# A forward and backward block on one core: one activation transpose, w_down's last part, the filter copy, the held matmuls and the last stores put at other places

## The chip, the cores and the metric

One core of a Trainium2 chip runs the whole program. The metric is the device time of one execution in microseconds (us). Shown are the median of three runs and one profiled execution, whose trace is the source of every row below. The engines are named as the profile names them: PE (TensorE, matmuls; PEld are its weight loads), DVE (VectorE), ACT (ScalarE), POOL (GpSimd) and SP (SyncE). SP and POOL issue nearly all DMAs here; SPq and POOLq are the issuing instructions in their queues. Each engine works through its own instruction list in a fixed order, and an instruction whose inputs or buffers are not ready holds up all behind it on that engine.

## The reference

The program computes an adaptive-layernorm block, forward and backward. With `x` of 2048 rows by 576, `h = norm(x)*(1+ca)+sa`; `x1 = x + ga*A(h)`, where A is a two-dimensional real FFT, a product with the complex filter `w_r + i*w_i`, and the inverse FFT; `h2 = norm(x1)*(1+cb)+sb`; `out = x1 + gb*B(h2)`, where B is the bilinear unit:

```python
g = jnp.einsum('bsd,df->bsf', x, w_gate)
u = jnp.einsum('bsd,df->bsf', x, w_up)
h = g * u
return jnp.einsum('bsf,fd->bsd', h, w_down)
```

The six vectors sa, ca, ga, sb, cb, gb are `silu(c) @ w_mod`. Outputs are `out` and the gradients of `x`, `w_r`, `w_i`, `w_gate`, `w_up`, `w_down`, `c` and `w_mod` for a given `grad_out`, all in bfloat16. F, the inner width of B, is 4608 = 36 blocks of 128; the 2048 rows are 16 tiles of 128.

## The kernel before

The kernel runs in stages that overlap at their edges.

*Forward stages* (to about 292 us of the span): norm, FFT as matmuls with tables, filter, inverse FFT, second norm; the matmuls for the gradient of the hidden layer are dealt between them.

*Block loop* (`for fb in range(NFB)`): for each of 36 blocks the products `gup` (gate and up), the elementwise `hhT`, `ggT`, `guT` (h, and its gradients toward gate and up), and their turned copies `hh_sf`, `gg_sf`, `gu_sf`, made by SP with a DMA transpose in `turn_items` (L684, L685). The turned copies feed `product(fb, i)` (`u57p`, L615): i = 0 is the gradient of w_down, i = 1 and 2 those of w_gate and w_up. Each finished product of w_gate or w_up is turned back through `woT` and stored by SP (`u57_turn`); one of w_down is stored by SP directly (L636). The pools of `sf` have two buffers each, so block 35 uses those of block 33. For block 35 the three transposes stand under `tc.high_priority(-2 * HEAD_START)`, that is, far back in the order in which the scheduler of the language deals instructions that are ready (`HEAD_START` is 350); elsewhere the offset is 0.

*Sums* (`u8_output`): the gradient of h2 for two blocks at a time, `u8p` (three banks), added by DVE into `acc` (L701).

*Held matmuls.* The products of blocks 34 and 35 (6 x 32 = 192 matmuls) are kept back and used as filler. `lead` deals 48 of them among the last sums, three per tile; `deal` gives the other 144, and then the projection matmuls of tiles 0 to 5 (`proj`, L1187), a fixed quota `q` in each step of the stages 1, 2 and 3, and `in_order` turns the list into PE's order. Held are in the order (34, 0), (35, 0), (34, 1), (35, 1), (34, 2), (35, 2).

*Stage 1* (`t1_norm`, `t1_turn`, `t1_cols`, `t1_rows`; 16 tiles, 19 steps): the backward of the second norm. Its loads `n2c`, `goc`, `yc` (L911) are issued by SP, five buffers each, with the tables RD, G1, BD2, BDA behind those of tiles 1 and 2. POOL stores each tile's `gxr` (L928, called gx below), and `queued_load` places one large POOL load behind a given tile's store: `wd_load` brings parts of w_down (`wdA` for blocks 0 to 14, then `wdB` three times seven blocks: 15, 22 and 29 on), `hl_load` parts of the stored hidden layer, `wn_load` the two halves of the filter copy. `queued` keeps these in the order written. The steps have the norm of tile k, the turn of k−1, the columns of k−2 and the rows of k−3, dealt in reverse.

*Stage 2* (`t2_*`, 19 groups, 24 steps): the backward through the filter. `t2_filter` multiplies with `wn` (`fm`, L214); its result `Ygc` is turned by PE (`try_`) two steps later. `filter_grad` makes the filter's gradient for a group, reading `Xn` (a POOL load, two buffers) and writing into `wn` in place; every fourth group runs in stage 2, the others later. *Stage 3* (`t3_*`, 18 steps): inverse transform and first norm.

*Projection* (16 tiles, the last loop): `u3p` = h by w_down, 72 matmuls per tile; ACT copies it (L1188), DVE makes `pr` (L1191), `of` (L1193) and the output `o` (L1195), POOL stores it (L1196). `x1t` and `got` are loaded by POOL for two tiles at a time, into one buffer each. Between the tiles stand the remaining filter gradients (`more_grads`), four stores of the filter's gradient per tile (`store_grads`, L1167) and the sections of the w_mod gradient (`late`, `section`). `csF` collects `pr` (two tiles late); after the last tile its copy `dgb` (L1214) feeds the last section and the gradient of c.

On chip the left-hand pools after the block loop lie where its buffers lay. Summed from the sizes, the last part of w_down (`oB2`, bytes 93,392 to 101,456 of this region in each partition) lies over the `gg_sf` and `gu_sf` pools, and the `hl` buffers of `hlh` and `hlg` over `h2p` and `gon`; the copy of the filter lies on the right, over `acc1`.

Of the kernel before, what the change touches and what calls it, by code (L numbers as in the profile page):

```python
# [31 lines left out]
HEAD_START = 350  # L32
# [52 lines left out]
def build(ctx, tc, A_x, A_w_r, A_w_i, B_w_gate, B_w_up, B_w_down, c_in, w_mod, grad_out,  # L85
# [3 lines left out]
    NFB = F // 128  # L89
# [24 lines left out]
    MSA, MCA, MGA, MSB, MCB, MGB = range(6)  # L114
# [446 lines left out]
    with ExitStack() as ms:  # L561
# [14 lines left out]
        with ExitStack() as bs:  # L576
# [100 lines left out]
            def turn_items(fb):  # L677
                def turns_():
                    hhT, ggT, guT = trip[fb][2:5]
                    nc.gpsimd.dma_start(hhT_d[:, :, fb, :].rearrange("tp f x -> f tp x"), hhT[:].rearrange("f (tp ti) p -> f tp (ti p)", ti=2))  # L680
                    sfs[fb] = []
                    for pool_, nm, srcT in zip(sfp, ("hh_sf", "gg_sf", "gu_sf"), (hhT, ggT, guT)):
                        sf = pool_.tile([128, NT, 128], BF, name=nm)
                        with tc.high_priority(-2 * HEAD_START if fb == NFB - 1 else 0):  # L684
                            turned = nc.sync.dma_start_transpose(out=sf[:], in_=srcT[:].rearrange("f t p -> f (t p)"))  # L685
                        sfs[fb].append(sf)
                    if fb % FBT == 1 and fb + 3 < NFB:
                        wTs[fb // FBT + 1] = wT_load(fb + 3, [turned.ins] * 5)
                return turns_
# [69 lines left out]
    with ExitStack() as ts:  # L759
# [56 lines left out]
        def deal(held, proj):  # L816
            more, seq = held + proj, list(lead)
            for n, (stage, k, ins) in enumerate(staged):
                seq += ins
                steps = sum(x[:2] == (stage, k) for x in staged)  # L820
                at = sum(x[:2] == (stage, k) for x in staged[:n + 1])
                if stage == 1:
                    q = 8
                else:
                    q = 12 if stage == 2 else 20 if k == 0 else 7
                q = q * at // steps - q * (at - 1) // steps
                seq, more = seq + more[:q], more[q:]
            in_order(seq)
# [32 lines left out]
        def of_rows(d):  # L861
            return [lambda h=h: spread(ones_f[:], d[:, h * 288:(h + 1) * 288]) for h in range(2)]

        def of_sums(d):
            return [lambda h=h: spread(sel[:, h, :], d[:]) for h in range(2)]
# [29 lines left out]
        with ExitStack() as r1:  # L895
# [9 lines left out]
            ld, gyTs, zts = {"order": []}, {}, {}  # L905
# [65 lines left out]
            dcb = diag_rows(tl, csA, csB, 288, "dcb")  # L971
# [22 lines left out]
        def wd_load(f0, n, behind_):  # L994
            k, w = wd_part(f0)
            queued(nc.gpsimd, behind_, w[:, f0 - k:f0 - k + n, :], B_w_down[f0 * 128:(f0 + n) * 128, :].rearrange("(j f) d -> f j d", f=128))
# [10 lines left out]
        def wn_load(c, behind_):  # L1007
            queued(nc.gpsimd, behind_, wn[:, c].rearrange("k a f -> k (a f)"), wn_d[:, c * NT * FP:(c + 1) * NT * FP])

        def queued_load(t, f, *args):  # L1010
            hl = f(*args, ld["gx", t])
            if t < NT - 1:
                in_order([last[nc.gpsimd], ld["gx", t + 1]])
            return hl
# [4 lines left out]
        first_hl = [queued_load(9 + nq, hl_load, nq, nc.gpsimd) for nq in range(3)]  # L1019
        queued_load(12, wd_load, 22, 7)  # L1020
        first_hl.append(queued_load(13, hl_load, 3, nc.gpsimd))
        for c in range(2):
            queued_load(14 + c, wn_load, c)
        wd_load(29, 7, None)
        fg = pool("fg", 2, "right", stack=rA)
        rB = ExitStack()
        A_ = planes(pool("rb", 1, "right", stack=rB), "j_A")
# [125 lines left out]
        rest = [ci for ci in range(NCH) if ci % 4]  # L1153

        def more_grads(t):
            for ci in rest[{5: 0, 7: 3, 9: 7, 11: 11}.get(t, 99):][:3 if t in (5, 11) else 4]:
                with tc.issue_after(ld3["last"]):
                    filter_grad(ci)
            if t == 11:
                for which in range(2):  # L1160
                    for f in (0, DF - 1):
                        nc.gpsimd.tensor_scalar(out=wn[:, which, :, f:f + 1], in0=wn[:, which, :, f:f + 1], scalar1=0.5, scalar2=None, op0=MUL)
# [3 lines left out]
            with tc.issue_after(ins):  # L1166
                nc.gpsimd.dma_start((o2_v, o3_v)[which][:, a0:a0 + 2, :], wn[:, which, a0:a0 + 2, 0:DF])  # L1167

        late = {6: (MSB, of_sums(dsb)), 8: (MCB, of_rows(dcb)), 10: (MGA, of_rows(dga)), 12: (MSA, of_sums(dsa)), 13: (MCA, of_rows(dca))}


        csF = ps_cs.tile([128, 512], FP32, name="csF", tag="csB")
# [1 line left out]
        for tp_ in range(NT // 2):  # L1174
            hls = [first_hl[q] if tp_ == 0 else hl_load(4 * tp_ + q) for q in range(4)]
            x1t = o2p.tile([128, 2, D], BF, name="x1t3", bufs=1)
            nc.gpsimd.dma_start(x1t[:], x1_d[:, 2 * tp_:2 * tp_ + 2, :])
            got = o2p.tile([128, 2, D], BF, name="got3", bufs=1)
            nc.gpsimd.dma_start(got[:], go_v[:, 2 * tp_:2 * tp_ + 2, :])
            for ti in range(2):  # L1180
                t = 2 * tp_ + ti
                mark = traced()
                ob = o2p.tile([128, D], BF, name="ob3")
                for h in range(2):
                    p2 = ps_u3.tile([128, 512], FP32, name="u3p")
                    for fb in range(NFB):
                        mm = nc.tensor.matmul(p2[:, 0:288], lhsT=hls[fb // 9][:, fb % 9, ti * 128:(ti + 1) * 128], rhs=wd_part(fb)[1][:, fb - wd_part(fb)[0], h * 288:(h + 1) * 288], start=(fb == 0), stop=(fb == NFB - 1))  # L1187
                    nc.scalar.copy(ob[:, h * 288:(h + 1) * 288], p2[:, 0:288])  # L1188
                pr = prs[t] = o2p.tile([128, D], BF, name="pr3", bufs=3)
                for h in range(2):  # L1190
                    nc.vector.tensor_tensor(out=pr[:, h * 288:(h + 1) * 288], in0=ob[:, h * 288:(h + 1) * 288], in1=got[:, ti, h * 288:(h + 1) * 288], op=MUL)  # L1191
                of = o2p.tile([128, D], BF, name="of3", bufs=1)
                nc.vector.tensor_tensor(out=of[:], in0=ob[:], in1=gb_h[:], op=MUL)  # L1193
                o0 = o2p.tile([128, D], BF, name="o03", bufs=1)
                nc.vector.tensor_tensor(out=o0[:], in0=of[:], in1=x1t[:, ti, :], op=ADD)  # L1195
                stored = nc.gpsimd.dma_start(o0_v[:, t, :], o0[:])  # L1196
                if t in late:
                    with tc.issue_after(mm.ins):
                        section(*late[t], secp)
                more_grads(t)  # L1200
                if 11 <= t < 15:
                    for k in range(4 * (t - 11), 4 * (t - 10)):
                        store_grads(k, stored.ins)
                if t == 0:
                    add_zero(csF, first=True)
                for d_ in ([t - 2] if t < NT - 1 else [t - 2, t - 1, t]):
                    for h in range(2):
                        if d_ >= 0:
                            colsum(csF, h, prs[d_][:, h * 288:(h + 1) * 288])
                proj[t] = pe_since(mark)  # L1210
# [78 lines left out]
```

## Time and profile before

| what | value |
|---|---|
| runs, median (lowest to highest) | 1581.1 us (1576.41 to 1584.73) |
| profiled execution, own time | 1585.44 us |
| its span | 1583.6 us |
| PE / DVE / ACT / POOL busy | 1516.1 / 1032.1 / 555.7 / 190.0 us |
| granted clock, mean | 0.984 |
| DMA moved | 280.19 MB, mean 177 GB/s |

The stages lie in the span about so: block loop to 1243, sums to 1279, stage 1 to 1347, stage 2 to 1413, stage 3 to 1476, projection to 1567, then the end. In the rows, the first number of a timeline row is its start in us from the span's start, the second its length; what stands in square brackets is the idle time of that engine before it and what ended it. "issue" there means that nothing the profile shows was waited for. A row "DMA to landing" counts from a transfer's issue to its arrival. A PE row's length is longer than the distance between its matmuls, since these are pipelined.

### The profile page before, as it was taken

Reading aid. Unit: us, or ns where it says so; the run is one execution under the profiler, and the core shown is the slowest. Engines: PE = TensorE matmul, PEld = TensorE weight load, DVE = VectorE, ACT = ScalarE, POOL = GpSimd, SP = SyncE. Lnnn points to the kernel's source line nnn. Section 1 sums busy time; section 2 is a strip of 40 time slices with the busy share of each in tenths; the row PEclk is TensorE's granted clock in tenths of the full one; section 3 lists DMA queues with packets and bytes.
Section 4 is the critical chain, followed back from the end, with each engine's and each line's share of the span. In section 5 each row is a group of like instructions: output and inputs, shape, how many; then the busy total and the mean of one; then the engine's idle time right before and its main releaser. Section 6 shows DMA issues by size and latency. Waiting matters only on the chain.

```text
span 1583.6 us, 30053 instructions
## 1 busy us (share of the span) xinstructions
PE 1516.1 (96%) x11300; PEld 1030.4 (65%) x11306; DVE 1032.1 (65%) x2622; ACT 555.7 (35%) x1141; POOL 190.0 (12%) x301
## 2 busy tenths in 40 slices
PE   6999989999999999999999999999999789799996
PEld 4665533567666666666666666666766567588774
DVE  7866743666666666666666666666666666578765
ACT  6667722322222222222222222222222246467222
POOL 0001212101010000101001010100100312210224
PEclk9999999999999999999999999999999989899998
DMA  9869998778877685785768777675866769654866
GB/s 316 275 196 242 285 212 230 151 149 144 151 147 154 128 168 115 158 157 118 161 135 155 144 151 132 146 162 117 161 128 129 203 170 291 173 198 146 304 209 166
DMA packets 488195, 280.19 MB, mean 177 GB/s; under 512 B 408913, under 2 KB 459218, under 8 KB 487026
## 3 DMA queue, kind: packets, MB, share of 16 engines
q1 hardware_dynamic: 460898, 177.69, 52.8%
q0 software_dynamic: 27152, 100.59, 21.7%
q8 instruction: 88, 1.44, 0.4%
q14 instruction: 57, 0.47, 0.1%
HBM read 108.33 MB, written 82.31 MB: 120 GB/s over the span
## 4 chain that ended last, share of the span: by engine, by line
PE 77%; DVE 7%; DMA 6%; issue 6%; ACT 2%; POOL 1%; SPq 1%; DVEq 0%; ACTq 0%; POOLq 0%
PE u57p L615 26%; PE u8p L696 17%; PE gup L667 16%; PE u4p L426 7%; PE gup L662 2%; PE u3p L1187 2%; DMA Xn<-xn_d 1%; DMA hh_sf<-hhT 1%; DMA wdB<-in_B_w_down_dram 1%; PE zp L952 1%; DVE pr L880 1%; PE zp L364 1%; DVE ln_st L162 1%; DMA x1t<-x_d 1%; DMA wdT<-wdn 1%
## 5 line engine op out<-in xcount | busy, mean ns | idle before, releaser
L701 DVE TENSOR_TENSOR acc<-acc,u8p 128x288 f32<-128x288 f32 x1088 | 489.2, 453 | 326.9 <-PE u8p L696 326.7
L696 PE MATMUL u8p<-wT,ggT 128*128 128x288 bf16 x1152 | 329.3, 287 | 1.8 <-DVE acc L701 1.8
L696 PE MATMUL u8p<-wT,guT 128*128 128x288 bf16 x1152 | 328.8, 287 | 0.0
L667 PE MATMUL gup<-h2T,wgu 128*128 128x512 bf16 x1152 | 294.9, 379 | 0.0
L617 ACT CAST so<-u57p 128x288 bf16<-128x288 f32 x216 | 86.0, 398 | 534.8 <-PE u57p L615 526.8
L615 PE MATMUL u57p<-gon,hh_sf 128*128 128x288 bf16 x1152 | 189.6, 287 | 10.6 <-DMA hh_sf<-hhT 10.6
L615 PE MATMUL u57p<-h2p,gg_sf 128*128 128x288 bf16 x1152 | 189.8, 286 | 0.0
L615 PE MATMUL u57p<-h2p,gu_sf 128*128 128x288 bf16 x1152 | 188.2, 286 | 0.0
L667 PEld LDWEIGHTS <-wgu 128*128 128x128 bf16 x1152 | 109.5, 98 | 98.8 <-issue 17.1
L696 PEld LDWEIGHTS <-ggT 128*128 128x128 bf16 x1152 | 113.0, 98 | 67.7 <-issue 14.0
L426 PE MATMUL u4p<-goT,wdT 128*128 128x512 bf16 x656 | 152.7, 382 | 0.6 <-DVE goT L398 0.5
L696 PEld LDWEIGHTS <-guT 128*128 128x128 bf16 x1152 | 113.1, 98 | 56.2 <-issue 2.5
L615 PEld LDWEIGHTS <-hh_sf 128*128 128x128 bf16 x1152 | 112.8, 98 | 39.6 <-DMA hh_sf<-hhT 11.2
L1187 PEld LDWEIGHTS <-hl 128*128 128x128 bf16 x1152 | 108.7, 98 | 36.5 <-issue 12.4
L615 PEld LDWEIGHTS <-gu_sf 128*128 128x128 bf16 x1152 | 112.3, 98 | 28.5
L615 PEld LDWEIGHTS <-gg_sf 128*128 128x128 bf16 x1152 | 112.1, 98 | 28.1
L669 ACT CAST gT<-gup 128x512 bf16<-128x512 f32 x144 | 84.4, 586 | 130.7 <-PE gup L667 130.7
L426 PEld LDWEIGHTS <-wdT 128*128 128x128 bf16 x656 | 61.6, 98 | 74.6 <-issue 10.3
L669 ACT CAST uT<-gup 128x512 bf16<-128x512 f32 x144 | 84.3, 585 | 73.5 <-PE gup L667 73.5
L1187 PE MATMUL u3p<-wdB,hl 128*128 128x288 bf16 x672 | 99.3, 288 | 11.1 <-DMA wdB<-in_B_w_down_dram 11.1
L680 POOL DMA_DIRECT2D hhT_d<-hhT x36 | 33.2, 921 | 481.9 <-DVE hhT L671 452.9
L152 ACT CAST ghh_st<-u4p 128x512 bf16<-128x512 f32 x88 | 50.8, 586 | 73.7 <-PE u4p L426 72.8
(362 smaller groups left out, 1701.9 us busy)
## 6 DMA issues: line engine op xcount, KB each, us to landing
ghhT_d<-ghh_st POOLq DMA_DIRECT2D x36, 512.0 KB, 4.5
ghh<-ghhT_d POOLq DMA_DIRECT2D x36, 512.0 KB, 7.5
hhT_d<-hhT POOLq DMA_DIRECT2D x36, 512.0 KB, 6.5
hl<-hhT_d SPq DMA_DIRECT2D x28, 576.0 KB, 6.5
out_dram<-woT SPq DMA_DIRECT2D x72, 128.0 KB, 2.0
wdn<-in_B_w_down_dram SPq DMA_DIRECT2D x18, 288.0 KB, 3.8
out_dram<-so SPq DMA_DIRECT2D x36, 144.0 KB, 2.7
wgu<-in_B_w_gate_dram SPq DMA_DIRECT2D x18, 256.0 KB, 3.2
```

The lines of the kernel that those rows point to most:

```text
L152: nc.scalar.copy(dst, src)
L162: nc.vector.bn_stats(out=st[:, t, h, :], in_=xt[:, t, h * 288:(h + 1) * 288])
L426: nc.tensor.matmul(pt[:], lhsT=wdTs[k][:, j, m, :], rhs=goT[:, 4 * sb4:4 * sb4 + 4, m, :], start=(m == 0 and n == 5), stop=(m == n - 1))
L615: mm = nc.tensor.matmul(pw[0][:, 0:288], lhsT=sf[:, t, :], rhs=rhs_n[:, t, h * 288:(h + 1) * 288], start=(t == 0), stop=(t == NT - 1))
L617: nc.scalar.copy(so[:, h * 288:(h + 1) * 288], pw[0][:, 0:288])
L662: nc.tensor.matmul(pts[-1][:], lhsT=wgu[r, 8, jw * 128:(jw + 1) * 128], rhs=h2T[r, 4 * sb4:4 * sb4 + 4, 4, :], start=True, stop=False)
L667: nc.tensor.matmul(pts[k][:], lhsT=wgu[:, 4 * wi_ + m, jw * 128:(jw + 1) * 128], rhs=h2T[:, ts_, m, :], start=False, stop=(m == 3))
L669: nc.scalar.copy((gT, uT)[wi_][:, ts_, :], pts[k][:])
L680: nc.gpsimd.dma_start(hhT_d[:, :, fb, :].rearrange("tp f x -> f tp x"), hhT[:].rearrange("f (tp ti) p -> f tp (ti p)", ti=2))
L696: nc.tensor.matmul(pu[:, 0:288], lhsT=l_, rhs=r_, start=(k == 0), stop=(k == len(mms) - 1))
L701: nc.vector.tensor_tensor(out=dst, in0=dst, in1=pu[:, 0:288], op=ADD)
L1187: mm = nc.tensor.matmul(p2[:, 0:288], lhsT=hls[fb // 9][:, fb % 9, ti * 128:(ti + 1) * 128], rhs=wd_part(fb)[1][:, fb - wd_part(fb)[0], h ...
```

## The change

Five places change.

1. In `turn_items`, the turn `hh_sf` of the last block no longer has the lowered priority; `gg_sf` and `gu_sf` keep it.
2. In `deal`, the quota of stage 1 is 11 per step for the first 13 steps, then 8 as before.
3. The POOL loads at the end of stage 1: the last seven blocks of w_down now stand behind the gx store of tile 14, where the first half of the filter copy was; both halves of that copy come behind the store of tile 15 and behind that load.
4. The last three filter gradients and the halving of the filter's edge columns are written at tile 10 instead of 11, and the four stores per tile at tiles 10 to 13 instead of 11 to 14.
5. The last two sections inside the loop are at tiles 11 and 12 instead of 12 and 13.

```diff
-                        with tc.high_priority(-2 * HEAD_START if fb == NFB - 1 else 0):
+                        with tc.high_priority(-2 * HEAD_START if fb == NFB - 1 and nm != "hh_sf" else 0):
...
                 if stage == 1:
-                    q = 8
+                    q = 11 if k < 13 else 8
...
         queued_load(12, wd_load, 22, 7)
         first_hl.append(queued_load(13, hl_load, 3, nc.gpsimd))
-        for c in range(2):
-            queued_load(14 + c, wn_load, c)
-        wd_load(29, 7, None)
+        queued_load(14, wd_load, 29, 7)
+        wn_load(0, ld["gx", 15])
+        wn_load(1, None)
...
-            for ci in rest[{5: 0, 7: 3, 9: 7, 11: 11}.get(t, 99):][:3 if t in (5, 11) else 4]:
+            for ci in rest[{5: 0, 7: 3, 9: 7, 10: 11}.get(t, 99):][:3 if t in (5, 10) else 4]:
...
-            if t == 11:
+            if t == 10:
...
-        late = {6: (MSB, of_sums(dsb)), 8: (MCB, of_rows(dcb)), 10: (MGA, of_rows(dga)), 12: (MSA, of_sums(dsa)), 13: (MCA, of_rows(dca))}
+        late = {6: (MSB, of_sums(dsb)), 8: (MCB, of_rows(dcb)), 10: (MGA, of_rows(dga)), 11: (MSA, of_sums(dsa)), 12: (MCA, of_rows(dca))}
...
-                if 11 <= t < 15:
-                    for k in range(4 * (t - 11), 4 * (t - 10)):
+                if 10 <= t < 14:
+                    for k in range(4 * (t - 10), 4 * (t - 9)):
                         store_grads(k, stored.ins)
```

## The prediction

> **What bounds the kernel now.** I read the waits of TensorE (PE) in the last third first, because its busy share is high everywhere, then cut the span at those waits.
>
> ```profile
> PE u3p L1187 <- DMA wdB<-in_B_w_down_dram: 11.1, 1, 11.1
> PE u57p L615 <- DMA hh_sf<-hhT: 10.2, 1, 10.2
> PE gcp L1225 <- DVE gcd L1221: 6.7, 1, 6.7
> PE spp L858 <- DVE dgb L1214: 4.4, 1, 4.4
> PE u8p L696 <- DVE acc L701: 1.8, 4, 0.7
> ```
>
> The columns are total us, number, longest. Two single waits on transfers, 10.2 and 11.1 us, stand out; the next two are the end of the program. In the windows cut at these waits (PE, PE weight loads, VectorE = DVE, ScalarE = ACT, POOL busy us; then granted clock, DMA share, GB/s):
>
> ```profile
> 1260.50:1270.75 10.25, 0.02 (x1) 0.03 (x2) 2.56 (x7) 0.40 (x1) 6.31 (x6) 0.70 1.03 250
> 1270.75:1279.30 8.55, 8.55 (x54) 6.17 (x55) 3.98 (x9) 0.00 (x0) 0.00 (x0) 0.76 0.20 35
> 1279.30:1346.90 67.60, 65.30 (x648) 52.33 (x649) 45.61 (x122) 42.25 (x99) 16.05 (x27) 1.00 0.83 251
> ...
> 1351.30:1362.40 11.10, 0.04 (x2) 0.01 (x1) 1.77 (x5) 0.28 (x1) 0.94 (x3) 0.59 0.89 200
> 1362.40:1412.90 50.50, 50.38 (x543) 42.50 (x544) 40.51 (x127) 33.20 (x67) 8.13 (x18) 0.95 0.43 146
> 1412.90:1476.00 63.10, 62.99 (x583) 51.89 (x584) 49.14 (x134) 39.16 (x102) 4.83 (x9) 1.00 0.66 213
> ...
> 1566.70:1583.60 16.90, 2.98 (x6) 1.44 (x6) 7.33 (x17) 3.18 (x5) 8.23 (x8) 0.55 0.30 97
> ```
>
> Outside the two waits PE is busy nearly always, so a wait removed is time removed. Each wait also costs something behind it: the clock is 0.76 for 8.55 us after the first (0.24 x 8.55 = 2.05 us lost) and 0.95 for 50.5 us after the second (0.05 x 50.5 = 2.5 us; the 0.59 of the wait itself costs nothing). Together the two are worth 12.3 and 13.6 us.
>
> **Part 1, hh_sf turned earlier.** SyncE's (SP's) queue explains the first wait:
>
> ```profile
> 1243.64 2.24 SPq L685 DMA_TRANSPOSE gu_sf<-guT  x1
> 1245.93 1.31 SPq L911 DMA_DIRECT2D n2c<-n_d  x2
> ...
> 1263.14 0.38 SPq L636 DMA_DIRECT2D out_dram<-so  x1
> 1263.56 3.43 SPq L685 DMA_TRANSPOSE hh_sf<-hhT  x1
> ```
>
> and the list of transfers from 1230 to 1400 us its landing time:
>
> ```profile
> hh_sf<-hhT SPq DMA_TRANSPOSE x1, 7.1
> ```
>
> The turn of hh_sf for block 35 is issued at 1263.56, behind 17 us of norm-stage loads, and lands 7.1 us later. At its normal priority it stands ahead of them: issued about 1245.9, when gu_sf has been issued, landed about 1253. PE wants it at 1260.5, so seven us of slack: the wait goes, −12.3. What is late next are the loads behind it. Each is issued 2.24 (gu_sf's issue) to 3.43 us (its own) later, and VectorE already waits for the first of each:
>
> ```profile
> 1250.97 0.82 DVE L809 SCALAR_TENSOR_TENSOR w<-gn,rstd2g,n2c 128x576 bf16<-128x576 bf16 x1 [0.38 <-DMA n2c<-n_d]
> ...
> 1253.59 0.46 DVE L812 TENSOR_TENSOR u<-u,goc 128x576 bf16<-128x576 bf16 x1 [0.69 <-DMA goc<-in_grad_out_dram]
> ```
>
> Behind L809 on VectorE's queue stand the additions L701 that free the three banks u8p; PE waits for those already (the 1.8 us above), so a later n2c goes through to PE nearly whole. Bounds: 0 if the additions are dealt ahead of the norm, 7.1 if the loads land a whole turn later. I take 2.8, the middle of 2.24 and 3.43. The tables behind them (RD, G1, BD2, BDA) come later by the same 2 to 3 us, and are first read by the columns of stage 1, two steps after PE has left the sums; the turn of gg_sf keeps its place, since the queue's total is the same: nothing for either. Net **−9.5**.
>
> The Trainium skill, "DMA: Bandwidth & Descriptors", section "Queues, rings and completion order", says that on one DMA engine the descriptors of one queue row are consumed in ring order. By that the loads start only when the turn's packets are through, and the 7.1 would apply rather than 2.8: the first rival below.
>
> **Part 2, w_down's last part and the filter copy.** GpSimd's queue (POOL) and PE at the places that decide:
>
> ```profile
> 1330.57 0.54 POOL L928 DMA_DIRECT2D gx_d<-gxr  x1 [3.01 <-DVE gxr L814]
> 1331.10 0.54 POOL L989 DMA_DIRECT2D wn<-wn_d  x1
> ...
> 1334.67 0.55 POOL L928 DMA_DIRECT2D gx_d<-gxr  x1 [2.46 <-DVE gxr L814]
> 1335.20 0.54 POOL L989 DMA_DIRECT2D wn<-wn_d  x1
> ...
> 1346.87 0.97 POOL L989 DMA_DIRECT2D wdB<-in_B_w_down_dram  x1 [10.60 <-PE vp L960]
> ```
>
> ```profile
> 1327.82 0.41 PE L615 MATMUL u57p<-h2p,gu_sf 128*128 128x288 bf16 x2
> ...
> 1343.32 0.53 PE L615 MATMUL u57p<-h2p,gu_sf 128*128 128x288 bf16 x3
> ...
> 1345.92 0.65 PE L615 MATMUL u57p<-h2p,gu_sf 128*128 128x288 bf16 x4
> 1346.41 0.29 PE L959 MATMUL vp<-zt,T_G 128*128 128x292 bf16 x1
> ```
>
> wdB's last buffer takes the place of the gu_sf buffers (by the sizes of the left-hand pools), so its load must wait for the last held matmul: 1346.41 and then the usual POOL delay of 0.3 (named after L960, which ended then). At 8 per step, 152 places in 19 steps hold the 144 held matmuls and 8 projections. At 11 for k < 13, 143 are gone after step 12, the last one falls where the row at 1327.82 stands, and 47 projections follow in stage 1. The load, now behind the gx store of tile 14, is issued where the first wn copy was, 1331.1. It is first read by block 29: 7 + 8 + 8 = 23 projections precede step 16, whose third part holds blocks 28 to 30, the place of the row at 1343.32. That leaves 12.3 us. Landing times (three loads of wdB, then two of wn):
>
> ```profile
> DMA to landing us min/median/max: 8.0/8.2/15.5
> ...
> DMA to landing us min/median/max: 6.1/6.8/7.5
> ```
>
> Two of three fit; at 15.5 the wait would be 3.2 and the slow clock half of that again. A third of 3.2 is 1.1, my charge (bounds 0 and 4.8). Net 1.1 − 13.6 = **−12.5**.
>
> The wn copies are now issued at 1335.2 and 1335.7; 2 x 1168 KB (2.39 MB) at the 251 GB/s of this stage is 9.5 us, 1345.2. Their reader:
>
> ```profile
> 1350.70 0.76 DVE L214 TENSOR_TENSOR fm<-b_Vp,wn 128x512 bf16<-128x512 bf16 x2 [3.10 <-ACT b_Vp L1067]
> ```
>
> So 5.5 us in hand: 0, hidden by the end of stage 1; if the cover is gone, the rival below. POOL holds the gx store of tile 15, wn and the Xn loads behind wdB; none waits, as the held matmuls end first. Stage 2 then starts without the pause in which ScalarE and VectorE could run ahead; VectorE is at 40.5 of 50.5 us there, so little: +0.5 (0 to 2).
>
> **Part 3, 39 more matmuls in stage 1** (3 x 13). One costs (1346.41 − 1345.92) / 4 = 0.123 us, so 4.8 us of work moves ahead; what fills idle PE is gained. Stage 1 has 67.6 − 65.3 = 2.3 us idle; bounds 0 and 4.8 (busy counts overlap): **−2.3**. The list they are dealt from ends sooner: 152 + 288 + 139 = 579 places for 585 matmuls before, 618 now, so the last 33, about five steps of stage 3, have no filler named. That is 33 x 0.123 = 4.1 us of PE time, unless matmuls of tile 6, which no list holds back, step in. VectorE (49.1 of 63.1) would not stop them: **+1.0** (0 to 4.1).
>
> **Part 4, the last gradients, sections and stores a tile sooner.** The end:
>
> ```profile
> 1557.20 0.55 POOL L1177 DMA_DIRECT2D x1t<-x_d  x1
> 1568.03 0.55 POOL L1196 DMA_DIRECT2D out_dram<-o  x1 [10.28 <-issue]
> 1568.58 2.85 POOL L1167 DMA_DIRECT2D out_dram<-wn  x4
> ...
> 1566.14 0.50 PE L839 MATMUL csF<-pr,pick 128*128 128x288 bf16 x2 [0.78 <-DVE pr L1191]
> ...
> 1570.18 0.46 DVE L1195 TENSOR_TENSOR o<-of,x1t 128x576 bf16<-128x576 bf16 x1 [3.51 <-DMA out_dram<-o]
> 1570.55 0.45 DVE L1214 COPY dgb<-csF 128x288 f32<-128x288 f32 x1
> ```
>
> PE is done at 1566.6, but dgb stands behind the last L1195, which waits for the store issued at 1568.03. POOL's wait before it has no cause shown; tile 13's four wn stores and the loads and stores of a section are in flight then. The section goes 10 us away, the four stores after it vanish, but tile 13 still has four. At most 1570.55 − 1566.64 = 3.9 can go; I take half, **−2.0** (0 to −3.9). Against it, VectorE is late at tile 10:
>
> ```profile
> 1514.15 0.40 ACT L1188 CAST ob<-u3p 128x288 bf16<-128x288 f32 x1 [7.28 <-DVE of L1193]
> ```
>
> PE did not wait there, and the gradients named for tile 11 already run around it; 0, at worst +2.
>
> **Sum.** −9.5 − 12.5 + 0.5 − 2.3 + 1.0 − 2.0 = −24.8. The profiled execution took 1585.4 us (span 1583.6), the median of the runs is 1581.1, 4.3 lower. 1585.4 becomes 1560.6; the median 1581.1 becomes **1556**.
>
> **Rivals.** (a) *The loads behind hh_sf become the wait.* For: VectorE already waits for them and PE for VectorE. Against: the wait was only 0.38 and 0.69 us. 7.1 in place of 2.8, and as much as 2 more of VectorE's backlog in the norms of tiles 1 and 2: +6, **1562**. 15%.
>
> (b) *wdB still late, wn behind it.* For: the 15.5, in company of two hl loads and the last woT turn, which all start at the same event again. wdB lands at 1346.6 (+4.8 − 1.1), wn 9.5 us later at 1356.1, while PE needs the first filtered group near 1353: +3. In all +6.7, **1563**. 12%.
>
> (c) *The turn stays where it is* because the order on SP is worked out otherwise. Then −9.5 is lost: **1566**. 6%. (d) *The missing fillers and tile 10 both cost*: +3.1 + 2 + 2 (no gain at the end): **1563**. 8%.
>
> (e) *Slower: a bundle at the lowest rate.* In the wait of before, DMA moved little:
>
> ```profile
> 1350.00:1358.00 8.00, 1.33 (x14) 0.97 (x12) 2.37 (x6) 1.17 (x2) 0.00 (x0) 0.71 1.06 103
> ```
>
> If wdB (1.03 MB), two hl (1.18) and wn (2.39), 4.6 MB from 1328 on, all moved at 80 GB/s, wn would land 57 us later at 1385, 32 after its need and 2.5 of slow clock: −24.8 + 34.5 = +10, **1591**. It decides from about 92 GB/s (50 us) down. Against: 251 GB/s over stage 1, 103 only for 8 us. 3%.
>
> **How the numbers follow.** The forecast has 56%, its own range 1547 to 1566. What a measurement can tell from no change is about 0.5%, 8 us. Range 1544 to 1570: the lower end has the gains of parts 1, 3 and 4 nearly whole, the upper holds (a) to (d) and two mixed. Faster by over 8 us: 0.92, same 0.05, slower 0.03.
>
> **What would show it.** No wait of PE for hh_sf; a hh_sf issue before 1250; n2c waits of 2 to 3 us on VectorE in their place; wdB issued within 1 us of gx 14, with a PE wait under 2 us; 0.98 or more clock in the stages after; fm not waiting for wn; dgb within 2 us of the last csF. A PE wait of over 5 us at any of these, or for wn, would make the forecast wrong.

## The result, and the profile after

The changed kernel takes 1571.35 us (median of 13 runs), the kernel before, on the same chip, 1584.51 (13 runs, 1576.41 to 1597.93). The ratio is 0.991, with a 95% interval from 0.988 to 0.994: the change is faster by more than a measurement can miss, but gains about 13 us of the 25 that were forecast. The profiled execution has a span of 1568.7 us and a time of 1570.48. One run each of the change (1610.53 us, granted clock 0.942), of e7 and of e10 was over 1.5% slower than the fastest of its kernel; the ratios, and the medians of e7 and e10, are without it.

A single span says little about this change. The first of the held matmuls (it reads the hh_sf of block 34), ahead of which nothing of the program is changed, starts anywhere between 1235.7 and 1250.0 us in the 14 executions profiled for this study. So the span is cut from that matmul on, at the first trp (start of the norm stage), the first trv (start of stage 2, the filters), the first upa (start of stage 3; stage 3 and the projection are one stretch here, called projection) and the end of the last u3p (its start and 0.3 us). The column "forecast" has its terms put into the same stretches: −9.5 and 0.4 for three matmuls; 36 matmuls or 4.4, −2.3 and 1.1; −13.6 and 0.5; −4.8 for 39 matmuls and 1.0; −2.0.

| us | before | forecast | after | difference | after, less forecast |
|---|---|---|---|---|---|
| sums of the last block | 36.4 | 27.3 | 30.2 | −6.2 | +2.9 |
| norm stage | 67.3 | 70.5 | 73.7 | +6.4 | +3.2 |
| stage 2 | 65.4 | 52.3 | 51.9 | −13.5 | −0.4 |
| projection | 151.6 | 147.8 | 153.6 | +2.0 | +5.8 |
| tail | 18.7 | 16.7 | 13.6 | −5.1 | −3.1 |
| all of it | 339.4 | 314.6 | 323.0 | −16.4 | +8.4 |

The two large waits are gone. The waits of TensorE after (total us, number, longest):

```profile
PE gcp L1225 <- DVE gcd L1221: 6.7, 1, 6.7
PE u8p L696 <- DVE acc L701: 5.5, 4, 4.4
PE u3p L1187 <- ACT ob L1188: 5.1, 2, 2.6
PE trp L933 <- DVE b_Vp L154: 2.3, 1, 2.3
PE spp L858 <- DVE dgb L1214: 0.7, 1, 0.7
```

Where hh_sf (10.2) and wdB (11.1) stood, there are now waits for three other things (acc, ob and b_Vp), each in one of the three stretches that fell short. The windows of the five stretches after (us, busy PE, weight loads, DVE, ACT, POOL; granted clock, DMA share, GB/s; the first window starts 1 us ahead of the first held matmul) show a clock below 1.00 in these three, as at the end:

```profile
1244.75:1275.88 31.13, 25.51 (x188) 19.02 (x187) 23.25 (x61) 4.27 (x10) 12.49 (x10) 0.95 0.96 253
1275.88:1349.59 73.71, 70.88 (x685) 56.71 (x683) 47.80 (x127) 43.25 (x100) 21.11 (x36) 0.98 0.94 267
1349.59:1401.50 51.91, 51.91 (x582) 44.30 (x580) 41.60 (x130) 34.88 (x71) 8.39 (x17) 1.00 0.56 189
1401.50:1555.10 153.60, 148.30 (x1240) 118.16 (x1239) 105.21 (x278) 60.13 (x143) 30.33 (x51) 0.99 0.72 222
1555.10:1568.70 13.60, 3.06 (x14) 1.35 (x11) 8.01 (x19) 3.59 (x6) 4.83 (x3) 0.77 0.18 60
```

Stage 2 is full (51.91 of 51.91 us busy, clock 1.00): part 2 did there what it says, though the filter copy had nothing in hand. POOL and VectorE at that copy:

```profile
1335.33 0.55 POOL L928 DMA_DIRECT2D gx_d<-gxr  x1 [4.94 <-DVE gxr L814]
1341.82 0.54 POOL L783 DMA_DIRECT2D gb_h<-modb_d  x1 [5.94 <-ACT b_Vp L152]
...
1343.03 1.08 POOL L989 DMA_DIRECT2D wn<-wn_d  x2
...
1353.03 0.43 DVE L214 TENSOR_TENSOR fm<-b_Vp,wn 128x512 bf16<-128x512 bf16 x1 [0.24 <-DMA wn<-wn_d]
```

Ahead of wn in POOL's queue stands a small load, gb_h, that waits 5.94 us. So wn goes out at 1343.03, and not right behind the gx store of tile 15 at 1335.33, and VectorE waits 0.24 us for it: the 5.5 us that were to be in hand are used up, though TensorE does not notice.

**The sums.** SyncE's queue in the timeline after, and the rows of VectorE and TensorE that follow from it:

```profile
1245.19 2.70 SPq L685 DMA_TRANSPOSE gu_sf<-guT  x1
1247.99 4.79 SPq L685 DMA_TRANSPOSE hh_sf<-hhT  x1
1252.83 1.05 SPq L911 DMA_DIRECT2D n2c<-n_d  x2
...
1256.61 0.82 DVE L809 SCALAR_TENSOR_TENSOR w<-gn,rstd2g,n2c 128x576 bf16<-128x576 bf16 x1 [4.47 <-DMA n2c<-n_d]
...
1257.85 0.28 PE L696 MATMUL u8p<-wT,ggT 128*128 128x288 bf16 x1 [4.37 <-DVE acc L701]
```

hh_sf goes out at 1247.99, ahead of the loads as forecast, but takes 4.79 us to issue behind gu_sf, and the first n2c goes out 7.6 us after the first turn instead of 2.3. VectorE waits 4.47 us for it (0.38 before), and TensorE 4.37 for VectorE.

**The end of the norm stage.** SyncE, VectorE and TensorE after:

```profile
1314.06 1.22 SPq L625 DMA_TRANSPOSE woT<-so  x1
...
1316.46 0.40 SPq L911 DMA_DIRECT2D yc<-y_d  x1
1322.06 0.39 SPq L626 DMA_DIRECT2D out_dram<-woT  x1
...
1323.13 0.53 SPq L911 DMA_DIRECT2D n2c<-n_d  x1
...
1332.56 0.82 DVE L809 SCALAR_TENSOR_TENSOR w<-gn,rstd2g,n2c 128x576 bf16<-128x576 bf16 x1 [3.42 <-DMA n2c<-n_d]
...
1333.82 0.69 PE L933 MATMUL trp<-ident,gxr 128*128 128x128 bf16 x5 [2.35 <-DVE b_Vp L154]
```

A turn of the output weights is issued at 1314.06 and can be stored 8 us later; for the last 5.2 of these SyncE issues nothing. The last tile's n2c is queued behind that store, and once issued it takes 9.3 us to land, against 4.9 for the first n2c of before. wdB's last load takes 16.8 us (the longest of three):

```profile
DMA to landing us min/median/max: 8.1/8.7/16.8
```

**The projection.** ScalarE at the sections of tiles 10 to 12 (its copies ob free the projection's accumulators), and TensorE:

```profile
1519.55 0.70 ACT L152 COPY dmb<-spp 128x288 f32<-128x288 f32 x2 [9.28 <-DVE pr L880]
...
1530.46 0.70 ACT L152 COPY dmb<-spp 128x288 f32<-128x288 f32 x2 [6.55 <-DVE pr L880]
...
1534.36 2.24 ACT L887 ACTIVATE o<-dmb,sc_col 128x576 bf16<-128x576 f32 x3 [3.21 <-DMA out_dram<-o]
...
1523.66 2.54 PE L1187 MATMUL u3p<-wdA,hl 128*128 128x288 bf16 x15 [2.58 <-ACT ob L1188]
...
1537.08 2.00 PE L1187 MATMUL u3p<-wdA,hl 128*128 128x288 bf16 x15 [2.52 <-ACT ob L1188]
```

There is one buffer dmb. A section's copy into it waits until VectorE has finished the products of the section before; with sections at 10, 11 and 12 that is 9.28 and 6.55 us in which ScalarE does nothing, with TensorE's ob copies queued behind. The length of that wait alone does not make the stall: before, ScalarE waited 7.02 us ahead of the section at tile 13, and TensorE 1.0 for ob. In the second case here ScalarE also waits 3.21 us for the store of the section's output `o`, which has one buffer too.

### The profile page after: what moved, and what is told of

The parts are those of the page before. It is cut to its first block, busy times and chain, and to the rows that moved or that the text cites. A ratio compares the mean times of both kernels' runs of the same rounds, so it can differ in the third digit from the quotient of the medians.

```text
span 1568.7 us, 30057 instructions
## 1 busy us (share of the span) xinstructions
PE 1517.0 (97%) x11306; PEld 1030.6 (66%) x11306; DVE 1032.0 (66%) x2622; ACT 556.5 (35%) x1141; POOL 190.5 (12%) x301
## 4 chain that ended last, share of the span: by engine, by line
PE 85%; DMA 7%; DVE 4%; issue 2%; ACT 1%; SPq 1%; POOL 0%; DVEq 0%; ACTq 0%; POOLq 0%
PE u57p L615 27%; PE u8p L696 18%; PE gup L667 16%; PE u4p L426 7%; PE u3p L1187 4%; PE gup L662 3%; PE yp L197 2%; DMA Xn<-xn_d 2%; DMA wdT<-wdn 1%; DMA wdB<-in_B_w_down_dram 1%; PE zp L952 1%; DMA out_dram<-o 1%; PE zp L364 1%; PE upa L191 1%; DMA xc<-in_A_x_dram 1%
## 5 line engine op out<-in xcount | busy, mean ns | idle before, releaser
L615 PEld LDWEIGHTS <-gg_sf 128*128 128x128 bf16 x1152 | 112.4, 98 | 28.2
L1187 PE MATMUL u3p<-wdA,hl 128*128 128x288 bf16 x480 | 73.1, 289 | 5.1 <-ACT ob L1188 5.1
```

What stands on the lines that cost most here:

```text
L615: mm = nc.tensor.matmul(pw[0][:, 0:288], lhsT=sf[:, t, :], rhs=rhs_n[:, t, h * 288:(h + 1) * 288], start=(t == 0), stop=(t == NT - 1))
```

## Experiments: the parts alone

Six kernels take the change apart. The part that each keeps is shown by its added lines; "..." stands where lines or parts of a line are left out.

**Part 1 alone (e1).**

```
+ with tc.high_priority(-2 * HEAD_START if fb == NFB - 1 and nm != "hh_sf" else 0):
```

> The kernel before with the first edit alone (hh_sf of the last block at normal priority). Theory of the prediction: PE's 10.2 us wait for hh_sf and its 2 us of slow clock go, n2c comes 2 to 4 us later, the stretch from the first matmul of the sums to the first trp shrinks from 37.4 us by 9.5. Rival, from the trace after: two turns now stand ahead of the loads, the second takes over 4 us to issue, n2c comes over 5 us later than in the kernel before, PE waits about 4 us for the additions with a slow clock behind it, and the stretch shrinks by 6 to 7 us. Both: the wait of 11 us for wdB stays. Ratio 0.994 (prediction) or 0.996 (rival).

1578.29 us, ratio 0.997 (0.995 to 0.9995). The sums take 30.9 us against 36.4, with a wait of 4.2 us for acc (4.4 in the change), so this cost belongs to part 1 and needs nothing else of the change. The wait for wdB also fell, to 4.4 us, because that load landed in 8.9 us at most here instead of 15.5. Why is open; e3, whose loads there are the same, waits 9.8 us.

**Parts 2 and 3 alone (e2).**

```
+ q = 11 if k < 13 else 8
...
+ queued_load(14, wd_load, 29, 7)
+ wn_load(0, ld["gx", 15])
+ wn_load(1, None)
```

> The kernel before with the quota of 11 and the new order of the POOL loads, without the other edits. Prediction: no wait for wdB over 2 us, none in stage 1; from the first trp to the first trv 67.3 us becomes about 69.5 (36 more matmuls, of which 2.3 us fill idle PE), stage 2 12 us shorter: ratio 0.992. Rival, from the trace after: the held matmuls end while stage 1 still loads, two hl loads, the last woT turn, x1t, got and wdB start together, the n2c load of tile 15 takes 9 us instead of about 5, and PE waits 2 to 3 us in stage 1 with 1.7 of slow clock: 73 to 74 us there, ratio 0.993. If that wait is missing here but not in the kernel after, it hangs on the later loads of the first edit instead.

1577.09 us, ratio 0.9945 (0.991 to 0.998). Stage 2 falls from 65.4 to 52.0 us, as in the whole change. The norm stage rises to 75.3, and this time not for n2c: TensorE waits for wdB there.

```profile
PE u57p L615 <- DMA hh_sf<-hhT: 10.7, 1, 10.7
...
PE u3p L1187 <- DMA wdB<-in_B_w_down_dram: 4.2, 1, 4.2
```

**Part 4 alone (e3), and everything but the sections' places (e4).** e3 has the gradients, the sections and the stores a tile sooner; e4 is the whole change with

```
- late = {... 11: (MSA, of_sums(dsa)), 12: (MCA, of_rows(dca))}
+ late = {... 12: (MSA, of_sums(dsa)), 13: (MCA, of_rows(dca))}
```

> The kernel before with the edits of the projection alone (gradients, sections and stores a tile sooner). Prediction: 2 us faster, PE does not wait in the projection, ratio 0.999. Rival, from the trace after: sections at tiles 10, 11 and 12 follow each other without a tile between, ScalarE's copies of u3p stand behind copies of dmb that wait for the section before, PE waits twice 2.5 us for them with about 1.8 us of slow clock, and the end after the last u3p is 5 us shorter: 2 us slower in all, ratio 1.001.

> The kernel after with the last two sections back at tiles 12 and 13, gradients and stores left a tile sooner. If the sections make PE's waits for ob, those are gone and the stretch from the first upa to the last u3p is 146 to 147 us instead of 153.3; if the stores or gradients make them, they stay. If the stores make the shorter end, the end after the last u3p stays near 13.6 us; if the sections do, it goes back toward 18.7. Ratio to before 0.986 (sections make the waits, stores the end), 0.990 (neither, or the end is lost).

e3: 1586.1 us, ratio 1.001 (0.999 to 1.004): the part gives nothing. Its tail is 13.5 us, 5.2 shorter, but the projection grows from 151.6 to 161.8. The window where that happens (e3; the granted clock is the third figure from the end):

```profile
1536.00:1556.00 20.00, 15.44 (x99) 10.72 (x98) 12.14 (x33) 4.97 (x10) 8.53 (x14) 0.83 0.91 236
1556.00:1576.00 20.00, 17.95 (x133) 13.78 (x133) 7.25 (x20) 3.45 (x8) 7.90 (x13) 0.91 0.61 179
```

e4: 1564.85 us, ratio 0.990 (0.984 to 0.996). Its projection takes 148.1 us, its tail 18.1. So what the sections' new places win at the end (4.5 us against the whole change) they lose in the projection (5.5 us; in e3, 10.2 more than before). e4's norm stage, 69.8 us, is the only one with the change's quota and load order in which TensorE waits for no late transfer.

**Parts 2 and 3 singly (e8 and e11).**

> Of the whole change only the 11 held matmuls per step for the first 13 steps; the loads keep the order of before, so that w_down's last part is issued behind both parts of wn and gb_h. Theory (the held matmuls and the load order need each other: the matmuls reach w_down's last part some 10 us sooner, the load does not): TensorE waits 8 to 15 us for wdB near the end of the norm stage, as long as before, nothing is gained, 1582 to 1588 us. Rival (more held matmuls are worth their 2.3 us alone, and the wait for wdB shrinks since less of the list is left): wait under 8 us, 1574 to 1580.

> Of the whole change only the order of the loads (w_down's last part behind tile 14's gx, wn behind tile 15's), with 8 held matmuls per step as before. Theory (wdB's buffer is free only behind the last matmul on hh's old halves, which the slower list reaches at its old time, at the end of the norm stage): POOL stands at wdB until about 100 us after the first sums, tile 15's gx and wn queue up behind it, TensorE waits for wdB as long as before (9 to 12 us) and somewhat longer for what needs wn or gx: 1584 to 1590 us. Rival (the load goes out as soon as it is in the queue): the wait for wdB falls below 3 us and the time to 1570 to 1575, and the 11 held matmuls per step are worth nothing of part 2.

e8, with the 11 per step and the old order: 1585.28 us, ratio 1.001 (0.999 to 1.003). TensorE comes to wdB sooner, the load does not: in POOL's queue it stands behind wn and gb_h, and gb_h waits 12.33 us there.

```profile
PE u3p L1187 <- DMA wdB<-in_B_w_down_dram: 14.8, 1, 14.8
```

e11, the order with 8 per step: 1591.88 us, ratio 1.004 (1.001 to 1.007), slower. POOL stands 14.12 us at the load for the last held matmul, and what is queued behind that load goes out later still:

```profile
1352.56 0.97 POOL L989 DMA_DIRECT2D wdB<-in_B_w_down_dram  x1 [14.12 <-PE vp L960]
```

TensorE waits 9.7 us for wdB, and 4.3 for the first filtered group. VectorE comes late to that group: it waits 7.99 and 4.22 us for the last turn of the output weights and its store, and 1.39 for wn, whose second half stands behind gb_h, which waits 11.73. Each half alone is worth nothing or less; together (e2) they take 13 us off stage 2 and put 8.0 on the norm stage, where 4.4 us of the matmuls now stand.

## Experiments: what the three new waits come from

**The turn ahead of the loads (e5).** The whole change, with gu_sf held behind gg_sf, so that one turn and not two stand ahead of the norm loads (the arguments that stay are left out):

```
- with tc.high_priority(...):
+ with tc.high_priority(...), (tc.issue_after(turned.ins) if fb == NFB - 1 and nm == "gu_sf" else ExitStack()):
```

> The whole change, and beside it only the order of two turns on SyncE's queue: the last gu_sf is issued behind the norm loads again (after gg_sf), so that hh_sf stands alone ahead of them; every other engine's order is that of the changed kernel. Theory A (the loads are late because two turns, not one, stand ahead of them, and the second takes twice its time to issue): the first n2c load is issued 2 to 3.5 us after the first turn starts instead of 7.6, TensorE's wait for acc in the sums stretch falls from 4.4 to at most 1 us and its half clock goes, the stretch from the first matmul on hh_sf to the first trp falls from 30.2 to 25-27 us, and the time is 1565 to 1568 us. Rival B (the turn's packets slow the loads behind it, whatever the issue order): the first n2c takes 1 to 3 us longer from issue to landing than the 4.5 of before, the wait for acc stays 3 us or more, and the time is 1570 to 1573. Theory A's danger: gu_sf, issued last, is late for the held matmuls of the norm stage, which would show as a TensorE wait for gu_sf.

1565.74 us, ratio 0.989 (0.985 to 0.993). SyncE in e5, and the first wait for acc:

```profile
1240.91 2.23 SPq L685 DMA_TRANSPOSE hh_sf<-hhT  x1
1243.20 2.89 SPq L911 DMA_DIRECT2D n2c<-n_d  x2
...
1250.05 0.28 PE L696 MATMUL u8p<-wT,ggT 128*128 128x288 bf16 x1 [1.94 <-DVE acc L701]
```

n2c goes out 2.3 us after the turn, the longest wait for acc is 1.9 us, no matmul there runs at half clock, and the sums take 26.9 us: 3.3 less than in the change, and no wait for gu_sf appears. The order on the queue is shown to be the cause: in the six kernels with this order (e5, e6, e7, e9, e10, e12) the sums take 26.9 to 28.2 us, in the three with both turns ahead (the change, e1, e4) 30.2 to 31.3. The whole time cannot show it, as the intervals of e5 and of the change overlap. The expected "at most 1" for the wait was too good, and the five waits still total 4.1 us.

**The sections (e6 and e7).** Both are e5 with other places for the sections: e6 has them at 6, 8, 10, 12, 13 (the line of e4), e7 at 6, 7, 8, 10, 12 (the line is shortened to the tiles and sections):

```
- late = {6: MSB, 8: MCB, 10: MGA, 11: MSA, 12: MCA}
+ late = {6: MSB, 7: MCB, 8: MGA, 10: MSA, 12: MCA}
```

> e5 with the last two sections back at tiles 12 and 13 (gradients and stores stay a tile sooner). Theory A for the projection (the two waits for ScalarE's ob copies come from sections at 10, 11 and 12, each waiting for the one before it to give dmb free): those waits go (at most 1.5 us in all), the projection is 4 to 6 us shorter than in e5, the tail after the last u3p is 4 to 5 us longer, so the time is within 2 us of e5's, or 1 to 4 below it where the slow clock behind the waits counts. Rival (the waits come from the gradients' and stores' earlier places): the waits for ob stay at 4 us or more, and with the longer tail the time is 3 to 5 us above e5's.

> e5 with the sections at tiles 6, 7, 8, 10 and 12: the end stays at 12 as in the change, the crowding moves to tiles 6 to 8, ahead of the gradients' stores. Theory A (sections one tile apart hold up ScalarE through the one dmb buffer, wherever they stand): dmb copies at tiles 7 and 8 wait 6 us or more for VectorE's products, TensorE waits 3 to 5 us for ob there, and the time is about e5's (within 2 us). Rival (it is the w_mod loads, late among the gradients' stores of tiles 10 to 13, that hold the products up): at tiles 6 to 8 nothing waits over 1 us for ob, the tail is 13 to 14 us, and the time is 5 to 8 us below e5's.

e6: 1564.95 us, ratio 0.987 (0.984 to 0.990); projection 147.5 (e5 153.1), tail 17.6 (13.5): 1.5 us better in sum, within the 2 that were expected to be no difference. TensorE's wait for ob is 0.9 us there, so the gradients and stores, which stay a tile sooner, do not make it. e7: 1563.67 us, ratio 0.986 (0.983 to 0.990); projection 146.5 and tail 13.6, both gains at once, 6.5 us better than e5 in these two stretches, though the medians differ by 2.1 only (e7's norm stage took 76.5 us in its profile). Neither theory of e7 came out whole. Who waits for VectorE's products, and what they wait for, in e5 (first) and e7, in the view of the tile wmj, the part of w_mod that a section loads (the line with DMA is the time that the products waited for the load; total us and number):

```profile
  DMA wmj<-in_w_mod_dram: 5.3, 2
who waited for it (us, times):
  ACT dmb L152: 18.1, 3
```

```profile
  ACT dmb L152: 6.8, 2
```

At tiles 6 to 8 sections one tile apart still wait for the one buffer, 6.8 us in two waits, but the w_mod loads come in time, and TensorE never waits for ob. At tiles 10 to 12 both add up, and the load is itself late for want of a buffer: wmj has one, and in the change its load goes out at 1519.47, when the products of the section before have ended (1519.44). Two sections a tile apart (12 and 13, e6) hardly stall TensorE, three at 10 to 12 do, three at 6 to 8 do not. That the late loads and the store of `o` make the difference is argued, not shown: a second buffer, which would tell, was not tried.

**The end of the norm stage (e9, e10, e12).** e9 is e7 with the loads x1t and got of the first pair of tiles behind wn on POOL; e10 is e9 with six n2c buffers; e12 is e7 with got directly behind wdB and x1t behind wn.

```
e9:  + with behind(... if tp_ == 0 else []): nc.gpsimd.dma_start(...)
e10: - bufs=5
     + bufs=6 if k == "n2c" else 5
e12: + for dst, src in ((x1t, x1_d), (got, go_v))[::-1 if tp_ == 0 else 1]:
     +     with behind(behind_wd if tp_ == 0 else []): nc.gpsimd.dma_start(...)
```

> e7, and the first pair's two loads x1t and got (0.59 MB together, the first read on VectorE only behind the norm stage) issued on POOL behind both parts of wn instead of between the last norm tiles. Theory (the loads of the last microseconds of the norm stage share the DMA engines: in five of six profiled executions with the new load order TensorE waits there, for w_down's last part or for gxr behind a late n2c): with 0.59 MB fewer in that window w_down's last part lands in 13 us or less instead of 15.8 to 17.2, TensorE's waits for wdB and for b_Vp between the first and the last trp and the first trv are at most 1.5 us together, the stretch from the first trp to the first trv is 69 to 71 us instead of 72.8 to 76.5, and the time is 1558 to 1562 us. Rival (the two pairs hl on SyncE and the turn of so make the jam, the 0.59 MB are a small part): w_down's last part still takes 15 us or more, a wait of 3 us or more remains, time within 2 us of e7's 1564.

> e9 with six buffers instead of five for n2c, so that every n2c load goes out a tile sooner and the last tile's is landed before w_down's last part starts; one more n2c load goes out in the first batch, behind the 2 others before goc. Theory: VectorE no longer waits for n2c in the norm stage's last tile, in this and in every execution; stretch 69 to 70 us; the sixth load, 0.4 us of SyncE, costs the sums stretch 0 to 0.5; the time is 0 to 3 us below e9's. Rival (the n2c waits were chance and the sixth load delays the five goc behind it): sums stretch longer by 1 us or more, time up to 2 us above e9's.

> e7, and of the first pair's two loads got is issued on POOL directly behind w_down's last part (and the two Xn), x1t behind wn. In e9, where both stood behind wn, w_down's last part landed in 9.8 us and TensorE no longer waited for it, but got came 6.5 us late for VectorE's first product of the projection, b_Vp stood behind that product, and TensorE waited 4.6 us at the first trv. Theory (that wait is e9's own and the load order of the norm stage's end costs nothing else): got is landed before the first product, or at most 1.5 us late, w_down's last part lands in 13 us or less, the stretch from the first trp to the first trv is 69 to 71 us, and the time is 1555 to 1560 us. Rival (0.3 MB of got in the window are enough to jam w_down's last part again): it lands in 15 us or more, TensorE waits 2 us or more for it, stretch 72 to 75 us, time 1561 to 1565.

e9: 1561.49 us, ratio 0.987 (0.983 to 0.991). Landing times of wdB's three loads, and VectorE, in e9:

```profile
DMA to landing us min/median/max: 7.4/8.3/9.8
...
1341.48 0.31 DVE L1191 TENSOR_TENSOR pr<-ob,got 128x288 bf16<-128x288 bf16 x1 [6.47 <-DMA got<-in_grad_out_dram]
```

With x1t and got ahead of it, wdB's last load takes 12.5 to 17.2 us to land in six profiles (the change, e2, e4 to e7); behind it, 9.8, 8.7 and 8.5 (e9, e10, e12). So these two loads slow it, which is shown; whether by their 0.59 MB or by their place in POOL's queue is not. But the supposition that got is read only behind the norm stage was wrong. The product `pr` of the first projection tile, whose matmuls are dealt into this stage, stands on VectorE ahead of the last b_Vp and waits 6.47 us for got, and TensorE waits 4.6 us for that b_Vp. The stretch is 74.1 us, not 69 to 71; that the time fell into its range is luck.

e10: 1564.39 us (1553.93 to 1574.41), ratio 0.987 (0.982 to 0.992), no gain over e9. In its profiled execution, whose norm stage takes 82.1 us, a turn of the output weights could be stored only 15 us after its issue; SyncE issued nothing for the last 11.5 of these, and VectorE waited 3.94 and 3.61 us for n2c all the same:

```profile
1302.93 1.37 SPq L625 DMA_TRANSPOSE woT<-so  x1
...
1317.95 0.39 SPq L626 DMA_DIRECT2D out_dram<-woT  x1
```

The deeper buffer does not help a load that stands in the queue behind a store that waits. e12: 1561.42 us, ratio 0.985 (0.982 to 0.988), the lowest of the study, though the intervals of e4 to e7, e9 and e10 overlap it; wdB lands in 9.1 us at most, and got comes in time. Its norm stage is 72.5 us, not 69 to 71, because the next transfer is late, the store of the turned weights, for which the copy to dsb waits:

```profile
1343.71 0.46 DVE L974 COPY dsb<-csB 128x288 f32<-128x288 f32 x1 [4.80 <-DMA out_dram<-woT]
```

## Why the prediction was right or wrong

The forecast of 1556 us is too low by 15. Of that, 3.4 us is the base: the median of before is 1584.51 over 13 runs, not 1581.1 over three. The rest is gain that did not come. By the table above, three terms of the sum fell short: "0, at worst +2" for the projection in part 4 (5.8 us in that stretch), the charge of 1.1 for the end of the norm stage in part 2 (3.2), and the 2.8 for the loads in part 1 (2.9). The end of the program gained 3.1 more than forecast and hides some of this. The 8.4 us of the table are most of what is missing; the held matmuls also start 1.5 us later in the profile of the change than in that of before, and the rest lies between single profiles and medians.

**Part 1 (−9.5): mechanism right, one term mis-sized.** The wait for hh_sf went with its slow clock, −12.3. The term that failed is "I take 2.8, the middle of 2.24 and 3.43" for the loads behind it. Measured: 36.4 − 12.3 + 0.4 makes 24.5 us, the stretch took 30.2, so they cost 5.7. TensorE's waits for acc rose by 3.7 us (1.8 to 5.5), and the clock of 0.95 over 31.13 us is another 1.6. The loads were to be issued 2.24 to 3.43 us later; counted from the first held matmul, n2c goes out 1.8 us behind it before and 7.1 in the change, 5.4 later. The turn's issue, 3.43 us in the one row that the prediction took, was 4.79 in its new place, directly behind gu_sf. That the row was a good case could be seen in the trace of before, where hh_sf is turned 36 times, mostly directly behind gu_sf (ns to issue, least, median and most):

```profile
L685 SPq DMA_TRANSPOSE hh_sf<-hhT x36: 2293/6066/10119, 292.1 to 1263.6; - x36
```

The landing of the turn ahead of n2c is a second account of the same delay. From transfers and timelines:

| | last turn lands | n2c read |
|---|---|---|
| before | 1243.64 + 5.7 = 1249.3 | 1250.97 |
| after | 1247.99 + 8.3 = 1256.3 | 1256.61 |
| e5 | 1240.91 + 6.6 = 1247.5 | 1248.81 |
| e2 | 1244.48 + 4.3 = 1248.8 | 1251.82 |

The Trainium skill, "DMA: Bandwidth & Descriptors", section "Queues, rings and completion order", has descriptors consumed in ring order on each engine. These rows agree: in none of the 14 profiles is n2c read ahead of the turn's landing. With two turns ahead it is read 0.3 to 0.4 us behind the second one (the change, e1, e4), which in the change lands 5.4 us behind the first (1245.19 + 5.7 = 1250.9). But n2c does not always wait for it: in e2 and e3 the turn lands after 4.3 us, and n2c is read 3.0 and 3.1 us behind it, no sooner than before. Later issue and later landing are both 5.4 us, near the 5.7, and no run tells them apart. Rival (a), given 15%, was the nearer account of this stretch: its price of 7.1 was 1.4 above the 5.7, the forecast's 2.8 was 2.9 below.

**Part 2 (−12.5): right for stage 2, wrong for what runs beside it.** Stage 2 fell by 13.5 (forecast −13.1), and e8 and e11 show that the quota and the order are one part. The step that failed is the sentence "POOL holds the gx store of tile 15, wn and the Xn loads behind wdB; none waits" together with a landing time for wdB from the list of before. wn did wait, behind gb_h, which the prediction doesn't name. It came just about in time (VectorE waits 0.2 to 1.4 us for it in the change, e4, e5 and e6, TensorE at most 0.2), so that this cost nothing is luck. The price for wdB was right, its chance was not: TensorE waits 3.3 to 4.2 us for it in e2, e5 and e7, where 3.2 was priced and counted at "A third", and the last load took 14.7 to 17.2 us in five of six profiles of that order. The list of before was made where these transfers did not run side by side. With the held matmuls ahead, wdB, three hl, x1t, got, Xn, a turn and n2c start within some seven us, and DMA's share over the last 30 us of the stage rises from 0.86 to 0.97. The share alone doesn't decide: e4, where TensorE waits for none of them, has 1.07 there. What is late differs from run to run (n2c in the change and e6; wdB in e2, e5, e7; none in e4), and the charge of 1.1 stands against 3.0 to 6.7 us in five of six profiles of that order, taken against e4's 69.8. Removing one late transfer made another late (got in e9, a store in e12). What stays open is why e4 escapes, and the lowest that this stretch can reach with all of them in it.

**Part 3: right, as far as one profile shows.** e4 needs 69.8 us for 36 more matmuls (4.4 us) in a stage that took 67.3: 1.9 us of idle time filled, forecast 2.3. The charge of +1.0 for 33 places without a filler was not needed: the projection of e2, e8 and e7 is 146.5 us, 5.1 below before, where the 39 matmuls are worth 4.8.

**Part 4 (−2.0): two sizes off.** The tail gained 5.1, beyond its bound of 3.9, as the wait for dgb fell by 3.7, that for csF by 0.6, and the clock rose from 0.59 to 0.77. The projection lost 7.1 against e7's 146.5 where "0, at worst +2" was set down: 5.1 in the two waits for ob, and 1.8 by the clock of 0.91 in the 20 us around them (1520 to 1540). That step looked at VectorE at tile 10, and TensorE was indeed not stopped by it directly; what stopped it was ScalarE, in whose queue three sections came to stand one tile apart, with one buffer of each kind for all of them. Rival (d) had a price of the right kind (+2 at tile 10) for another reason.

Of the signs named, two did not come true in the profile of the change: "n2c waits of 2 to 3 us" was 4.47, and fm waited for wn, by 0.24 us. None of them looked at ScalarE's order or at the loads that wdB would meet, and no wait at them was over the 5 us that were to make the forecast wrong; four of 2.3 to 4.4 did.

## What to carry to other kernels

A wait that is removed lets everything behind it start at once: list the transfers that will then start within a few microseconds and price each by a landing time from an equally full stretch, not by one from a half-empty one. Price a transfer moved ahead of others in its queue by all its cases in the trace, above all those with the same one directly ahead, and not by the one row at its old place. Read every instruction between two loads of a queue: a small one that waits holds the large one. Before two uses of a single buffer are moved closer together, look at the engine that has to wait between them, and at what else is in its queue.

## What the hardware showed that was not expected

The issue of a turn on SyncE's queue has no fixed price. In the kernel before, gu_sf, with no turn directly ahead, took 1.3 to 4.4 us (35 cases, median 2.0), hh_sf directly behind it 2.3 to 10.1 (27 cases, median 6.1), and gg_sf directly behind hh_sf 1.9 to 6.0 (36 cases, median 3.1). Why the middle one takes longest is open.

Short waits of TensorE differ in kind, and not by their length alone. In the change, the matmuls behind the wait of 4.37 us took 0.45 us instead of 0.28 until 1262.0, about 3.3 us, so the wait cost about a third more than its length; slow clock also followed the waits of 2.35 and 2.58 there and one of 2.25 in e5, but not that of 2.52. In e12 a wait of 1.58, with one of 0.56 behind it, was enough:

```profile
1260.57 0.28 PE L696 MATMUL u8p<-wT,ggT 128*128 128x288 bf16 x1 [1.58 <-DVE acc L701]
...
1262.85 0.44 PE L696 MATMUL u8p<-wT,ggT 128*128 128x288 bf16 x1
```

In e5 one of 1.94 and one of 3.27 were followed by no slow clock (no window of e5 between 1240 and 1500 us has less than 1.00):

```profile
1335.51 0.41 PE L1187 MATMUL u3p<-wdB,hl 128*128 128x288 bf16 x2 [3.27 <-DMA wdB<-in_B_w_down_dram]
```

What decides between 1.6 and 3.3 us no run here shows.
